# Seven conditional expert blocks, one after the other or one inside the other, on one core of Trainium2

## The chip, the core and the metric

The kernel runs on one core of one Trainium2 chip. A core has five engines with queues of their own: PE (TensorE, the matrix engine; PEld is its weight load), DVE (VectorE), ACT (ScalarE), POOL (GpSimd) and SP (SyncE). Each runs its own instruction list, and semaphores order them against each other. In this kernel SP issues the plain transfers; POOL issues the indirect ones, which take row numbers from a table. The metric is the device time in microseconds (us), the median of three runs; for the kernel before it is 813.92 us (813.45 to 814.21).

## The reference

Three layers on 4 x 576 = 2304 tokens of 512 numbers, in float32:

```python
q_s = softmax over the head dimension of q;  k_s = softmax over the sequence of k
kv = einsum('bhsd,bhse->bhde', k_s, v);  x = einsum('bhsd,bhde->bhse', q_s, kv)   # 4 x 8 heads x 64
x = (sigmoid(x @ w_gate) * (x @ w_val)) @ w_out                                   # 512 -> 1536 -> 512
logits = x @ w_gate2;  expert = argmax(logits);  gate = softmax(logits)[expert]   # 8 experts
# the first 576 tokens of an expert, in token order, are kept, the others give 0
out[i] = gate[i] * (relu(x[i] @ w1[expert]) @ w2[expert])                         # 512 -> 1024 -> 512
```

How many tokens an expert has is known only when the second layer is done. With the inputs used here four experts have tokens, and four have none.

## The kernel before

Every float32 product is made of three products of rounded parts (high x high, high x low, low x high), hence three matmul lines, 115 to 117, in the helper `mm3`, and "splits" (lines 134 and 135), in which ACT writes the rounded part and DVE or POOL the remainder.

The first two layers run over four blocks of tokens and write x to a buffer `x2d` in device memory. Beside the last block, tokens are routed: a table `tbl` in device memory holds, for each expert and slot, the token's number and its gate. POOL writes it with scatters (`scatter`, line 144), three for each block, the last three called by `rt["put"]()` in line 919. SP reads pieces of it back with `fetch` (lines 155 to 164).

The third layer is the subject. The expert with the most tokens goes first, outside any condition: 192 of its rows beside the last routing, then its last 384 rows. Their table is fetched into the tile `tb` by line 939, a step of the hidden chunk f = 3; the three scatters of the last block to the table are issued later, as one of the pieces in the list `weave`, which are called one by one between matmuls. The other seven follow in order of their number of tokens, each in a block of its own:

```python
for j in range(1, NE):
    with tc.If(nact > j):
        st, ew = body(j, st, ew)
```

`nact`, the number of experts that have tokens, is read by every engine from the tile `plan`. It is 4 here: the blocks j = 1, 2, 3 run, and j = 4 to 7 are passed over. `tc.If` makes a compare-and-branch on every engine, in the profile at line 1055. When the condition doesn't hold, the engine jumps to a small block that stands behind the body, the skip block: it waits for what the body before it left open, makes the semaphores' counts what they would be after the body (on POOL with INC_SWDGE_SEM), and branches on.

`body` (lines 1020 to 1052) multiplies 256 rows of one expert, and 320 more under an inner condition (line 1043), whose other side only splits weights. Inside, ACT makes the relu (line 235), DVE the low part of it (line 238), PE the second product into `yo`, ACT scales it by the gate (line 214), half tiles pass through a transfer to `z` (line 217), and POOL scatters the rows to the output (line 144). Beside this work SP loads the weights of the next expert into the staging tile `es` (lines 123 and 124), ACT, DVE and POOL split them into `eu`, SP fetches the next expert's table (lines 160 and 164), and POOL gathers its rows from `x2d` into `gr` (line 167).

Tiles come from pools: `hp` 4, `stg` 2, `psa` 5, `pso` 3, `grp` 7, `xgp` 2, `tbp` 2 of each kind; each call of `pool.tile` takes the next one and orders its users behind the last users of that place. The weights' `unit`s, six for an expert, are taken anew in every body. The program ends at line 1094, which is the closing barrier.

Of the kernel before, what the change touches and what calls it, by code (L numbers as in the profile page):

```python
# [8 lines left out]
F32 = mybir.dt.float32  # L9
F32R = mybir.dt.float32r  # L10
# [8 lines left out]
P = 128  # L19
# [19 lines left out]
SKIP = 8192  # L39
SPE = [mybir.EngineType.SP]  # L40

# The order in which the work up to the first pair of hidden chunks is issued, each engine's in turn: a step and
# what it is for (batch, tile or hidden chunk), with a star where VectorE takes it from its usual engine.
FIRST = """
lk0.0 lq0 km0.0 lk0.3 qm0 km0.3 lq3 ke0.0 ke0.3 lk0.2 qm3 lk0.1 qb0 qe0 kt0.3 km0.2 lk1 km0.1 lv0.0 ke0.2 qb3
qe3 lq1 qs0 qn0 kt0.0 lv0.3 kt0.2 ke0.1 kt0.4 qs3 km1.1 qt0 kc0.2 qn3 kc0.0 km1.2 kc0.4 kt0.1 kk0.0 kc0.3 qm1
# [21 lines left out]
go4.0 hl5.1* ac4.2 ac3.2* ac4.0*  # L68
"""
F64_MIN = struct.unpack("<f", struct.pack("<I", 897 << 20))[0]  # L70


def program(tc, ins, outs):
    nc = tc.nc
    ctx = ExitStack()
    with ctx:
# [76 lines left out]
            tc.add_to_no_dep_group(group, i.ins)  # L153

        def fetch(st, key, e, r0, k, rest=False):
            """The table's rows from r0 on: k to a partition, the rest's last half tile in both halves."""
            st[key] = t = tbp.tile([P, k + rest, 4], I32, name=key, tag=key[:2])
            t3 = tbl.rearrange("(e r) w -> e r w", e=NE)
            r1 = r0 + k * P
            nc.sync.dma_start(t[:, :k], t3[bass.ds(e, 1), r0:r1].rearrange("o (p k) w -> (o p) k w", k=k))  # L160
            if rest:
                for h in (0, HALF):
                    rows = t3[bass.ds(e, 1), r1 : r1 + HALF].rearrange("o p w -> (o p) w")
                    nc.sync.dma_start(t[h : h + HALF, k], rows)
# [21 lines left out]
            )  # L186

        def part(x, w, sizes, ew, t, ypool, ytag, hook, after):
            """The rows of one table for one expert. The high and low parts of a tile of half the rows fill the
            array's columns together; the low part's sums then move to the high part's partitions."""  # L190
            k, used = len(sizes), sum(sizes)
            full = used // P * P
            po, ys = [None] * k, [None] * k

            def second(f, h, i):
                n, sl = sizes[i], slice(i * P, i * P + sizes[i])
                w_hi, w_lo = ew[1, f][:, 0], ew[1, f][:, 1]
                if f == 0:
                    po[i] = pso.tile([P, 512], F32, name=f"yo{i}", tag="o")
                if n == P:  # L200
                    mm3(po[i], h[:, 0, sl], h[:, 1, sl], w_hi, w_lo, f == 0, f == 7)
                    return
                if f > 0:
                    nc.tensor.matmul(po[i][:n], h[:, 0, sl], w_lo, start=False, stop=False)
                nc.tensor.matmul(po[i], h[:, 0, used - n : used + n], w_hi, start=f == 0, stop=f == 7)
                if f == 0:
                    nc.tensor.matmul(po[i][:n], h[:, 0, sl], w_lo, start=False, stop=False)
                if weave:
                    weave.pop(0)()

            def emit(i):
                n = sizes[i]
                y = ypool.tile([P, DM], F32, name=f"y{i}", tag=ytag)
                nc.scalar.activation(y, po[i], AF.Copy, scale=t[:, i, 2:3].bitcast(F32))
                if n < P:
                    z = unit([P, DM], F32, f"z{i}") if ytag == "cv" else ypool.tile([P, DM], F32, name=f"z{i}", tag=ytag)
                    nc.sync.dma_start(z[:n], y[n:])
                    yield
                    nc.vector.tensor_tensor(y[:n], y[:n], z[:n], op=ALU.add)
                scatter(outs["out"], t[:n, i, 1:2], y[:n], NT, "out")  # L220

            hs = []
            for f in range(8):
                hook(f)
                ph = ps(f"ph{f}")[:, :w]
                w4 = ew[0, f].rearrange("p l (c m) -> p l c m", c=NC)
                for j, (l, r) in enumerate(((0, 0), (1, 0), (0, 1)) if f == 0 else ()):
                    for c in range(NC):
                        nc.tensor.matmul(
                            ph, w4[:, l, c], x[:, c, r], start=j + c == 0, stop=j == 2 and c == NC - 1  # L230
                        )
                for c in range(NC if f else 0):
                    mm3(ph, w4[:, 0, c], w4[:, 1, c], x[:, c, 0], x[:, c, 1], c == 0, c == NC - 1)
                h = hp.tile([P, 2, BLK], F32R, name=f"h3{f}", tag="h")
                nc.scalar.activation(h[:, 0, :used], ph[:, :used], AF.Relu)  # L235
                for dst, cols in ((h[:, 0, used : 2 * used - full], slice(full, used)), (h[:, 1, :full], slice(0, full))):
                    if cols.start < cols.stop:
                        nc.vector.scalar_tensor_tensor(  # L238
                            dst, ph[:, cols], 0.0, h[:, 0, cols].bitcast(F32), op0=ALU.max, op1=ALU.subtract
                        )  # L240
                hs.append(h)
                if 0 < f < 7:
                    for i in range(k):
                        second(f - 1, hs[f - 1], i)
                if f < 7:
                    after(f)
            half = sizes[-1] < P
            order = ([k - 1] if half else []) + list(range(k - half))
            for i in order[:2]:
                second(6, hs[6], i)  # L250
            after(7)
            after(8)
            out = [emit(i) for i in range(k)]
            for j, i in enumerate(order):
                second(7, hs[7], i)
                next(out[i], None)
                if j + 2 < k:
                    second(6, hs[6], order[j + 2])
            next(out[-1], None)

        with ExitStack() as s2:
# [247 lines left out]
            otile = {}  # L509

            def g2(b, fs, mode):
                """mode: add (whole sums to SBUF), open and close (a sum over two pairs in PSUM)"""
                order = [(tt, i) for tt in range(TPB) for i in range(2)]
                if b == NBLK - 1 and mode == "close":
                    order = [(tt, 0) for tt in range(TPB)] + [(tt, 1) for tt in range(TPB)]
                for tt, i in order:
                    if i == 0 and mode != "close":
                        otile[b, tt] = pso.tile([P, 512], F32, name=f"po{b}_{fs[0]}_{tt}", tag="o")
                    pair(b, tt, fs[i], i, mode != "close" and i == 0, mode != "open" and i == 1)
                    if i == 1 and mode != "open":  # L520
                        nc.vector.tensor_tensor(row(b, tt), row(b, tt), otile[b, tt], op=ALU.add)  # L521
                if fs[-1] == NFC - 1:
                    finish(b)
# [49 lines left out]
            nsum = {0: (5, 5, 5), 1: (5, 5, 5), 2: (5, 5, 5), 4: (5, 5)}  # L573

            def logits(b):
                """Queues the logits of block b: DVE sums nsum[b] products of a row, Pool and ScalarE the others."""
                lg_tile(b)
                for tt, n in enumerate(nsum[b]):
                    qd.extend((b, tt, e) for e in range(n))
                    qg.extend((b, tt, e) for e in range(n, NE))  # L580

            def slot(room, spare):
                """Fills the time that DVE (room, in products) and Pool (spare) have until the next pair's turn."""
                lg_sum(0)
                put = None
                busy = {x[0] for x in qd + qg}
# [315 lines left out]
            def last_rows():  # L902
# [12 lines left out]
                def end():  # L915
                    nc.vector.tensor_tensor(gidx, pi[:, :3], st0["tb5"][:, :, 0], op=ALU.add)
                    for i in range(3):
                        gather(st0, 2 + i, gidx[:, i : i + 1], w5[:, 0, i], P)
                    rt["put"]()

                weave.extend([lambda: None] + [lambda k=k: one(k) for k in range(3)] + [end])

            def after0(f):
# [12 lines left out]
                if f == 3:  # L936
                    last_rows()
                    ew_split(ew0, 7, both)
                    fetch(st0, "tb", rt["e0"], R0, 3)
                if f == 4:  # L940
                    rt["plan"] = make_plan()
                if f >= 4:
# [74 lines left out]

        nact = st.pop("nact")

        def body(j, st, ew):  # L1020
            more = j + 1 < NE
            cj = nc.values_load(plan[0:1, NE + j : NE + j + 1], min_val=0, max_val=NT)
            xb = unit([P, NC, 2, RB], F32R, "xb")
            nst, new = {}, {}

            def extra(f):
                if f == 0:
# [9 lines left out]

            half = work(new, nexp[j], range(4), (2, 4, 5, 6)) if more else {}
            part(st["xa"], RA, (P, P), ew, st["ta"], grp, "gr", *hooks(half, extra))
            if more:  # L1040
                for k in (3, 4, 5):
                    new["u", k] = unit([P, 3, 2, 512], F32R, f"eu{k}")
            with tc.If(cj > RA) as big:  # L1043
                half = work(new, nexp[j], range(4, 8), (1, 3, 5, 6)) if more else {}
                part(xb, RB, (P, P, HALF), ew, st["tb"], grp, "gr", *hooks(half))
# [5 lines left out]
                            w()  # L1051
            return nst, new

        for j in range(1, NE):
            with tc.If(nact > j):  # L1055
                st, ew = body(j, st, ew)


def layout(inputs):
# [38 lines left out]
```

## Time and profile before

| what | value |
|---|---|
| median of three runs (lowest, highest) | 813.92 us (813.45, 814.21) |
| profiled execution: span | 815.9 us |
| profiled execution: own time beside its span | none given |
| PE busy | 757.5 us (93%) |
| PE weight load busy | 689.0 us (84%) |
| DVE busy | 474.4 us (58%) |
| ACT busy | 293.0 us (36%) |
| POOL busy | 321.0 us (39%) |
| bytes moved | 72.62 MB, mean 89 GB/s |

The page comes from one profiled execution, whose time is not given apart from its span; the span is 2.0 us above the median of the runs. Busy times count work only: branches, waits on semaphores and the issue of transfers are not in them. They stand in the views of a line under the names PEldq, DVEq, ACTq, POOLq and SPq, the engines' queues. The granted clock PEclk is a share of full speed: 1.00 is 2.4 GHz.

### The profile page before, as it was taken

To read this page: it belongs to the slowest core of one execution; us is meant where nothing else is said; L and a number is where in the kernel's file an instruction comes from. 1 tells how busy PE (TensorE), PEld (TensorE's weight loads), DVE (VectorE), ACT (ScalarE), POOL (GpSimd) and SP (SyncE) were. 2 spreads that over 40 slices of the span, in tenths; PEclk is the share of its full clock that TensorE was granted. 3 is DMA by queue.
4 is the path that set the end of the run, shared out by engine and by line. 5 is a ranking of instruction groups with operands and counts; after the bars stand their busy time and mean duration, and the time that the engine had idled before them with its cause. 6 is when DMAs were issued, how large, how long until landed. Compare 5 with 4: busy or idle time off the path is not lost. (4 is left out here: it accounts for less than half of the span.)

```text
span 815.9 us, 11856 instructions
## 1 busy us (share of the span) xinstructions
PE 757.5 (93%) x4268; PEld 689.0 (84%) x4268; DVE 474.4 (58%) x933; ACT 293.0 (36%) x592; POOL 321.0 (39%) x309
## 2 busy tenths in 40 slices
PE   6989999999999999999997898989999999999980
PEld 5988998999999999999886787978798888888870
DVE  7999956344545445546889895587624422533330
ACT  6766733222222222222333332233235433523330
POOL 5472703222323223223466763462435423425220
PEclk9999999999999999999999898999999999999995
DMA  9951023101101011011211011124245523415311
GB/s 308 365 174 58 27 78 130 57 26 52 50 29 52 28 50 52 27 53 51 79 39 40 1 39 40 53 91 144 66 146 189 177 78 125 155 53 176 129 46 30
DMA packets 34942, 72.62 MB, mean 89 GB/s; under 512 B 6544, under 2 KB 8720, under 8 KB 34736
## 3 DMA queue, kind: packets, MB, share of 16 engines
q1 hardware_dynamic: 31152, 61.50, 22.7%
q0 software_dynamic: 3712, 10.13, 3.8%
q8 instruction: 42, 0.69, 0.4%
q14 instruction: 36, 0.29, 0.1%
HBM read 61.55 MB, written 9.55 MB: 87 GB/s over the span
## 5 line engine op out<-in xcount | busy, mean ns | idle before, releaser
L491 POOL TENSOR_TENSOR h<-sg,h 128x384 fp32r<-128x384 f32 x70 | 77.7, 1111 | 200.8 <-ACT h L487 194.6
L483 DVE TENSOR_TENSOR sg<-sg,pv 128x384 f32<-128x384 f32 x72 | 39.6, 551 | 103.2 <-PE pv L117 78.5
L115 PE MATMUL po<-w,h 128*128 128x512 f32 x216 | 88.4, 409 | 10.9 <-ACT h L487 10.9
L117 PE MATMUL pv<-xT,w 128*128 128x384 f32 x288 | 97.1, 337 | 1.5 <-POOL w L451 1.5
L115 PE MATMUL pg<-xT,w 128*128 128x384 f32 x288 | 98.0, 340 | 0.0
L115 PE MATMUL pv<-xT,w 128*128 128x384 f32 x288 | 97.7, 339 | 0.1
L116 PE MATMUL pv<-xT,w 128*128 128x384 f32 x288 | 96.8, 336 | 0.0
L116 PE MATMUL pg<-xT,w 128*128 128x384 f32 x288 | 96.7, 336 | 0.0
L117 PE MATMUL pg<-xT,w 128*128 128x384 f32 x288 | 96.4, 335 | 0.0
L117 PE MATMUL po<-w,h 128*128 128x512 f32 x216 | 89.4, 414 | 4.5 <-POOL h L491 4.4
L116 PE MATMUL po<-w,h 128*128 128x512 f32 x216 | 87.6, 406 | 0.0
L238 DVE SCALAR_TENSOR_TENSOR h<-ph,h 128x64 fp32r<-128x64 f32 (+2 forms) x96 | 31.3, 353 | 94.6 <-ACT h L235 87.5
L451 POOL TENSOR_TENSOR w<-cv,w 128x512 fp32r<-128x512 f32 x34 | 45.0, 1324 | 98.7 <-ACT w L447 97.7
L487 ACT CAST h<-sg 128x384 fp32r<-128x384 f32 x68 | 34.9, 514 | 132.9 <-DVE sg L483 125.0
L135 POOL TENSOR_TENSOR eu<-es,eu 128x512 fp32r<-128x512 f32 x34 | 44.4, 1310 | 87.1 <-ACT eu L134 80.9
L521 DVE TENSOR_TENSOR acc<-acc,po 128x512 f32<-128x512 f32 x78 | 52.8, 686 | 34.7 <-PE po L117 32.7
L479 ACT ACTIVATE sg<-pg 128x384 f32<-128x384 f32 x72 | 35.0, 486 | 102.8 <-PE pg L117 102.8
L235 ACT ACTIVATE h<-ph 128x256 fp32r<-128x256 f32 (+3 forms) x64 | 26.3, 411 | 109.0 <-PE ph L117 54.4
L135 DVE TENSOR_TENSOR eu<-es,eu 128x512 fp32r<-128x512 f32 x46 | 48.3, 1061 | 26.3 <-ACT eu L134 26.0
L115 PEld LDWEIGHTS po<-w,h 128*128 128x128 f32 x216 | 42.0, 194 | 21.3 <-ACT h L487 13.5
L557 DVE CUSTOM_DVE_ANT_0 jk<-acc,wgb 128x512 bf16<-128x512 f32 x55 | 58.8, 1069 | 1.5
L117 PEld LDWEIGHTS po<-w,h 128*128 128x128 f32 x216 | 42.3, 196 | 17.3 <-POOL h L491 7.4
(206 smaller groups left out, 1804.1 us busy)
## 6 DMA issues: line engine op xcount, KB each, us to landing
es<-in_w SPq DMA_DIRECT2D x80, 256.0 KB
s<-in_w SPq DMA_DIRECT2D x30, 512.0 KB
q<-in_q SPq DMA_DIRECT2D x18, 256.0 KB
x2d<-acc SPq DMA_DIRECT2D x6, 768.0 KB
kt<-in_kT SPq DMA_DIRECT2D x3, 1152.0 KB
vt<-in_v SPq DMA_DIRECT2D x3, 1024.0 KB
raw<-in_w SPq DMA_DIRECT2D x6, 512.0 KB
wgb<-in_wg SPq DMA_DIRECT2D x1, 2048.0 KB
```

Source lines behind the costliest of these rows:

```text
L115: nc.tensor.matmul(out, l_hi, r_hi, start=start, stop=False)
L116: nc.tensor.matmul(out, l_hi, r_lo, start=False, stop=False)
L117: nc.tensor.matmul(out, l_lo, r_hi, start=False, stop=stop)
L135: engines[(i + f) % 2].tensor_tensor(u[:, 1], s[:, i], u[:, 0].bitcast(F32), op=ALU.subtract)
L238: nc.vector.scalar_tensor_tensor(dst, ph[:, cols], 0.0, h[:, 0, cols].bitcast(F32), op0=ALU.max, op1=ALU.subtract)
L451: two[eng].tensor_tensor(w[:, i, 1, :], ld.pop(("c", f, i))[0], w[:, i, 0, :].bitcast(F32), op=ALU.subtract)
L479: nc.scalar.activation(pr, gt.pop(("g", b, f)), AF.Sigmoid)
L483: nc.vector.tensor_tensor(pr, pr, gt.pop(("v", b, f)), op=ALU.mult)
L487: alt[eng](h[:, 0], gt["r", b, f])
L491: two[eng].tensor_tensor(h[:, 1], gt.pop(("r", b, f)), h[:, 0].bitcast(F32), op=ALU.subtract)
L521: nc.vector.tensor_tensor(row(b, tt), row(b, tt), otile[b, tt], op=ALU.add)
L557: nc.vector.tensor_tensor_reduce(junk, row(b, tt), rt["wg"][:, e, :], 1.0, 0.0, op0=ALU.mult, op1=ALU.add, accum_out=rt["lg", b][:, tt, e ...
```

## The change

Four things differ. (1) The seven blocks stand one inside the other: `chain` opens the condition of number j, writes its body and then, still inside, calls itself for j + 1. (2) The tiles of the third layer are taken once, ahead of the blocks, and come round as fixed lists (`Ring`, and `Tables` for the two kinds of table tile), as many as the pools had; the weight units are two fixed sets of six, used in turn; the tile for the later rows is `xb1`, always the same. (3) The fetch of the first expert's last table rows is moved from the step of chunk f = 3 to behind `rt["put"]()`. (4) Comments are gone, by which the line numbers move.

```diff
+class Ring:
+    def __init__(self, tiles):
+        self.tiles, self.n = list(tiles), 0
+
+    def tile(self, shape, dt, name, tag):
+        self.n += 1
+        return self.tiles[(self.n - 1) % len(self.tiles)]
+
+class Tables:
+    def __init__(self, ta, tb):
+        self.of = {"ta": ta, "tb": tb}
...
                         gather(st0, 2 + i, gidx[:, i : i + 1], w5[:, 0, i], P)
                     rt["put"]()
+                    fetch(st0, "tb", rt["e0"], R0, 3)
...
                     last_rows()
                     ew_split(ew0, 7, both)
-                    fetch(st0, "tb", rt["e0"], R0, 3)
...
+        def ring(pool, n, shape, dt, tag, *first):
+            more = [pool.tile(shape, dt, name=f"{tag}r{i}", tag=tag) for i in range(n)]
+            return Ring([*more, *first])
+        sets = [
+            {k: u for k, u in ew.items() if k[0] == "u"},
+            {("u", k): unit([P, 3, 2, 512], F32R, f"ev{k}") for k in range(6)},
+        ]
+        xb1 = unit([P, NC, 2, RB], F32R, "xb1")
+        hp = ring(hp, 4, [P, 2, BLK], F32R, "h")
+        stg = ring(stg, 2, [P, 2, 512], F32, "stg")
...
+        tbp = Tables(ring(tbp, 1, [P, 2, 4], I32, "ta", st["ta"]), ring(tbp, 1, [P, 3, 4], I32, "tb", st["tb"]))
...
-            xb = unit([P, NC, 2, RB], F32R, "xb")
-            nst, new = {}, {}
+            xb = xb1
+            nst, new = {}, dict(sets[j % 2])
...
-            if more:
-                for k in (3, 4, 5):
-                    new["u", k] = unit([P, 3, 2, 512], F32R, f"eu{k}")
...
-        for j in range(1, NE):
+        def chain(j, st, ew):
             with tc.If(nact > j):
-                st, ew = body(j, st, ew)
+                nst, new = body(j, st, ew)
+                if j + 1 < NE:
+                    chain(j + 1, nst, new)
+
+        chain(1, st, ew)
```

In the order of the instructions the change is seen at three places. The first is POOL's list where one of the seven blocks ends and the next begins. Before, there stand the last two splits of a body, the end of the inner condition, the skip block of the outer one (line 1055: one instruction of the kind that holds INC_SWDGE_SEM, and a branch), the compare of the next block and the first lines of its body. DMAHW, DMASW and names of engines are semaphores.

```order
L135 TENSOR_TENSOR eu_7868<-es_8137,eu_7868 128x512 [waits DMAHW6_49,Activation_49]
L1043 ISA [waits DMASW7_49,DMASW6_49,DMASW5_49]
L1043 UNCONDITIONAL_BRANCH
L1055 ISA [waits Pool_49,Pool_sequencer_49,DMASW4_49,DMASW5_49,DMASW3_49,DMASW6_49,DMASW2_49,DMASW7_49,DMASW1_49,DMASW0_49]
L1055 UNCONDITIONAL_BRANCH
L1055 COMPARE_AND_BRANCH
L1022 TENSOR_LOAD plan
```

And now, the end of POOL's list: the skip blocks of the nested conditions, those of the inner ones first, and behind them the closing barrier.

```order
L1089 ISA [waits Pool_49,Pool_sequencer_49,DMASW4_49,DMASW5_49,DMASW3_49,DMASW6_49,DMASW2_49,DMASW7_49,DMASW1_49,DMASW0_49]
L1089 UNCONDITIONAL_BRANCH
L1089 ISA [waits Pool_49,Pool_sequencer_49,DMASW4_49,DMASW5_49,DMASW3_49,DMASW6_49,DMASW2_49,DMASW7_49,DMASW1_49,DMASW0_49]
L1089 UNCONDITIONAL_BRANCH
L1132 ISA [waits barrier_Pool_Activation_PE_DVE_SP_gather]
```

The skip block, an ISA instruction and a branch, stood behind each body; now all seven stand together at the end of the list, two of them shown here.

The second place is PE's list. Before, where a body ends, its skip block (one branch with waits) and the next compare follow the last product.

```order
L116 MATMUL yo_7915<-eu_7291,h_8082 128x512
L117 MATMUL yo_7915<-eu_7291,h_8082 128x512
L1043 UNCONDITIONAL_BRANCH
L1043 UNCONDITIONAL_BRANCH [waits PE_49]
L1055 UNCONDITIONAL_BRANCH [waits PE_49,PE_sequencer_49]
L1055 COMPARE_AND_BRANCH
L1022 TENSOR_LOAD plan
```

Now, the end of PE's list, behind the last body's last product.

```order
L135 MATMUL or_5854<-eu_5806,hr_5846 128x512
L136 MATMUL or_5854<-eu_5806,hr_5846 128x512
L1077 UNCONDITIONAL_BRANCH
L1077 UNCONDITIONAL_BRANCH [waits PE_49]
L1089 UNCONDITIONAL_BRANCH [waits PE_49,PE_sequencer_49] x7
```

The seven branches that stood each behind its own body stand behind one another at the end.

The third place is SP's list around the moved fetch, where the first expert's 192 rows are multiplied: `es` are weights of an expert, `tb<-tbl` the fetch, and the load of `plan` follows it. Before:

```order
L124 DMA es_5096<-in_w 128x512
L160 ISA
L160 DMA tb<-tbl 128x12
L217 DMA z_5349<-y_5347 64x512 [waits Activation_49]
L973 TENSOR_LOAD plan [waits DVE_49]
```

Now:

```order
L143 DMA es_5096<-in_w 128x512
L179 ISA
L179 DMA tb<-tbl 128x12 [waits DMASW6_49]
L236 DMA z_5349<-y_5347 64x512 [waits Activation_49]
L992 TENSOR_LOAD plan [waits DVE_49]
```

On SP the fetch has kept its neighbours and has a wait for one of POOL's transfers.

## Rows read from the trace of the kernel before

**Rows 1.** first line of the page

```profile
span 815.9 us, 11856 instructions
```

**Rows 2.** stages: the bodies, the end (columns in the first line)

```profile
core 0: us, PE busy (x) PEld busy (x) DVE busy (x) ACT busy (x) POOL busy (x), PEclk, DMA share, GB/s
735.40:790.80 55.40, 54.52 (x326) 48.08 (x325) 19.56 (x38) 20.76 (x42) 20.27 (x18) 1.00 0.37 122
790.80:801.40 10.60, 2.27 (x10) 1.50 (x8) 0.68 (x1) 2.06 (x3) 2.90 (x3) 0.71 0.32 87
801.40:815.90 14.50, 0.00 (x0) 0.00 (x0) 0.00 (x0) 0.00 (x0) 0.00 (x0) 0.50 0.04 7
```

**Rows 3.** line 1055 from 790 us (ns min/median/max, start us)

```profile
L1055 PEldq COMPARE_BRANCH  x4: 4761/4855/4924, 790.9 to 806.5; - x4
...
L1055 POOLq COMPARE_BRANCH  x4: 45/48/50, 796.5 to 808.1; - x4
L1055 POOLq INC_SWDGE_SEM  x4: 1353/1353/1357, 801.5 to 808.8; - x4
```

**Rows 4.** line 1055 on POOL, four stretches from 797, 803, 806 and 808.2 us

```profile
L1055 POOLq EVENT_SEMAPHORE  x4: 17/43/43, 800.9 to 801.4; - x4
...
L1055 POOLq COMPARE_BRANCH  x1: 50/50/50, 802.8 to 802.8; - x1
...
L1055 POOLq EVENT_SEMAPHORE  x6: 17/30/43, 803.3 to 803.8; - x6
...
L1055 POOLq COMPARE_BRANCH  x1: 45/45/45, 805.2 to 805.2; - x1
...
L1055 POOLq EVENT_SEMAPHORE  x6: 17/30/43, 806.2 to 806.7; - x6
...
L1055 POOLq COMPARE_BRANCH  x1: 45/45/45, 808.1 to 808.1; - x1
...
L1055 POOLq EVENT_SEMAPHORE  x5: 17/43/43, 808.3 to 808.7; - x5
```

**Rows 5.** line 1094, the end of the program

```profile
L1094 SPq EVENT_SEMAPHORE  x14: 17/28/1201, 810.1 to 815.9; - x14
...
L1094 POOLq DRAIN  x3: 46/107/4960, 810.1 to 815.7; - x3
...
L1094 PEldq DRAIN  x2: 8/8/8, 811.8 to 815.4; - x2
```

**Rows 6.** end of the chain of work (start us, us, what)

```profile
796.59 0.92 POOL out L144
```

**Rows 7.** waits of SP's queue from 780 us (total, times, longest)

```profile
SPq L1094 <- PEq L1055: 1.2, 1, 1.2
```

**Rows 8.** DMA queues, 796 to 799.2, then 799.2 to 801 us

```profile
q0 software_dynamic: 122, 0.38, 39.8%
q8 instruction: 2, 0.03, 7.8%
...
q0 software_dynamic: 9, 0.02, 5.6%
```

**Rows 9.** line 1055 on DVE, 796.9 to 799.8 us

```profile
L1055 DVEq EVENT_SEMAPHORE  x3: 21/21/21, 796.9 to 799.5; - x3
L1055 DVEq COMPARE_BRANCH  x2: 56/56/56, 797.0 to 799.6; - x2
```

**Rows 10.** waits of PE in the three bodies, 624 to 791 us

```profile
PE yo L115 <- ACT h L235: 1.4, 2, 0.8
PE yo L115 <- issue: 0.9, 1, 0.9
```

**Rows 11.** tbl on POOL, z on SP, SP's waits, 580 to 640 us

```profile
L144 POOL DMA_INDIRECT tbl<-ent,si x3: 977/1005/1024, 585.0 to 587.7; - x3
...
L217 SPq DMA_DIRECT2D z<-y x1: 507/507/507, 592.1 to 592.1; - x1
...
SPq L217 <- ACT y L214: 19.1, 1, 19.1
```

More of the change, by code (lines that the diff above doesn't have):

```diff
@@ L70, with tile @@
 F64_MIN = struct.unpack("<f", struct.pack("<I", 897 << 20))[0]
+class Ring:
[7 more added lines that the diff above has]
+        self.of = {"ta": ta, "tb": tb}
+    def tile(self, shape, dt, name, tag):
+        return self.of[tag].tile(shape, dt, name, tag)
 def program(tc, ins, outs):
@@ L1018, in program @@
         nact = st.pop("nact")
+        def ring(pool, n, shape, dt, tag, *first):
[8 more added lines that the diff above has]
+        stg = ring(stg, 2, [P, 2, 512], F32, "stg")
+        psa = ring(psa, 5, [P, 512], F32, "a")
+        pso = ring(pso, 3, [P, 512], F32, "o")
+        grp = ring(grp, 7, [P, DM], F32, "gr")
+        xgp = ring(xgp, 1, [P, NC, 2, RA], F32R, "xa", st["xa"])
+        tbp = Tables(ring(tbp, 1, [P, 2, 4], I32, "ta", st["ta"]), ring(tbp, 1, [P, 3, 4], I32, "tb", st["tb"]))
         def body(j, st, ew):
```

## The prediction

> **What bounds the kernel now.** I read the stages first, then the end of the chain of work, then the branch line 1055 and the closing line 1094. The span is 815.9 us [rows 1]. In the expert bodies TensorE is the limit: the third body takes 55.4 us and PE is busy 54.5 of them at a granted clock of 1.00, which is 2.4 GHz, while the DMA engines are busy a third of the time [rows 2]. In all three bodies PE waits for ACT or for instructions 2.3 us in total [rows 10]. Whatever the change does inside a body has only these 2.3 us to win.
>
> The last 14.5 us, from 801.4 on, hold no compute at all: every engine's busy time is zero [rows 2]. The chain of work that ended last stops with the third output scatter of the last body, which starts at 796.6 and takes 0.9 us [rows 6]; everything after 797.5 is branches, waits and the closing barrier. There the reader sees four not-taken decisions of line 1055, each of them on PE and on POOL, so four of the seven experts are skipped and three run (one hot expert ahead of them) [rows 3].
>
> On POOL each skip is a few waits, one INC_SWDGE_SEM of 1.35 us and a branch. The first skip cannot begin before the scatters have landed: its waits end between 800.9 and 801.4 [rows 4]. The first of the four INCs starts at 801.5, the last at 808.8 [rows 3]. POOL then starts a DRAIN at 810.1, which is the 4.96 us one, so it ends at 815.1, and 0.8 us of barrier close the span [rows 5, 1]. TensorE needs 4.76 to 4.92 us for each of its four skips, because the branch itself takes that long [rows 3]; it reaches its own drain at 811.8 [rows 5], 3.3 us before POOL's DRAIN ends. So POOL's queue is the end of the kernel, PE's the next one behind it.
>
> **The change part by part.**
>
> Nesting. Compare number four still fails, its skip block runs, and the branch at the end of that block leads to the end of the program, past the skip blocks of numbers three, two and one. Three of four skips go, on all engines. On POOL from the start of the first INC (801.5) to the start of the DRAIN (810.1) is 8.6 us; of that 1.35 for one INC stay and the exit branch. What a branch costs on POOL until the next instruction: from 802.8 to 803.3, 0.5; from 805.2 to 806.2, 1.0; from 808.1 to 808.3, 0.2 [rows 4]. I take 0.3 for the exit. 8.6 - 1.35 - 0.3 = 7.0 us.
>
> The jump to the skip block becomes longer: before, POOL leaps over one body, now over four. The nearest row for a leap that leaves what is loaded is DVE's, whose branch at 797.0 is followed by the next event only at 799.4 or 799.5: 2.4 us [rows 9]; PE's dearest is 4.9 [rows 3]. POOL branches at 796.5 and could not go on before 801.4 anyway; 796.5 + 4.9 = 801.4. So between 0 and 2.4 us are hidden behind the landing of the scatters, and even PE's price just fits. Cost 0. If that cover were gone, up to 2.4 (estimate from DVE's row).
>
> The landing itself. From 796 to 799.2 the scatter queue moves 122 packets, beside two instruction packets (0.03 MB), which I put down to PE's second skip, since its four skips lie 5.2 us apart from 790.9 on [rows 3]; from 799.2 to 801 only nine stragglers are left [rows 8]. With PE's second skip gone, those two loads are gone at this place, while POOL's longer jump may put one in. If the stragglers were behind them, the wait ends near 799.5 instead of 801.4, 1.9 us earlier; if not, 0. I take 0.9, the middle, since the rows name no cause.
>
> The DRAIN. Four are not to be seen, only one long one (4.96 us) and two short ones (0.05 and 0.11) [rows 5]. If it is a fixed price of the first drain after indirect DMAs it stays; if it works off what four INCs left, three quarters or all of it goes. I take it as fixed, because each INC stands in the trace as finished before the next instruction. If it shrinks, SP is next: after POOL's last INC it has 14 event waits, 810.1 to 812.0, of which 1.2 were PE's skip [rows 5, 7], so 0.7 us, then the 0.8 of the barrier.
>
> PE. Its one remaining skip ends its long branch at 790.9 + 4.8 = 795.7 and its drain follows there, if the exit is cheap, or at about 800.6 if the exit costs another 4.9. Both are before POOL. SP, DVE and ACT have one skip left, too, and wait for POOL.
>
> The Trainium skill ("Runtime: NRT & Kernel Launch", Instruction fetch mechanics) says that prefetch is sequential and that a taken branch to a target outside the loaded window stalls until that code has been fetched. PE's branch of 4.8 us against POOL's 0.05 on the same line agrees with it [rows 3], and it speaks against nesting: every engine's jump now goes further. By that rule alone the exit could stall as well, which is the second rival below.
>
> Tiles taken once. The pools of stage 3 and the weight tiles become fixed lists. The same tiles are used in the same rotation (4, 2, 5, 3, 7, and two sets of six weight units), so the matrix work and the splits are unchanged; what changes is the list of semaphores before an instruction. SP's weight loads now wait for each half of the staging tile by itself, which can only be earlier than waiting for both. All this sits beside PE, which is busy 98% of a body. Bounds: all 2.3 us of PE's waits go, or three more such waits of 0.9 come [rows 10]. I take 0.
>
> The moved fetch. The last 384 rows of the first expert's table are fetched by SP where the three scatters to the table have been issued, and wait for them. The last scatter starts at 587.7 and takes 1.0 [rows 11]. Landing: from the output scatters above at most 801.4 - 797.5 = 3.9 us, so 592.6 at the latest; with the fetch's issue SP is free at 593.0 at the latest. What is queued behind it on SP is the z transfer at 592.1, for which SP sat waiting 19.1 us [rows 11], then the loads of the plan and the next expert's weights. The entries of the table are 16 bytes a row instead of 2 KB, so I expect the landing near 590 and no delay: 0, at worst 0.9. The fetched rows are used only where that expert's outputs are scaled, at its end. POOL's scatters lose a wait for the fetch that was over anyway.
>
> **Sum.** 7.0 + 0.9 + 0 + 0 = 7.9 us off the profiled span of 815.9: 808.0. The page gives no other time for that execution; the median of the three runs, 813.92, is 2.0 below the span. I take the difference over to the median: 813.9 - 7.9 = 806.0 us. Its own range is 804 to 808: landing 0 to 1.9, exit 0.1 to 1.0, bodies about 1 either way.
>
> **Rivals.**
>
> The DRAIN shrinks with the skips. For: it is longer than any other drain, and four INCs precede it. Against: the INCs look finished. Then the end is the last INC, 801.5 - 0.9 + 1.35 = 801.9, plus 0.7 and 0.8, and 0.2 for the short drain and the exit: 803.6 in place of 815.9, so 12.3 less: 801.6.
>
> The exit pays a fetch on POOL. For: PE's branches [rows 3]. Against: the skip blocks passed over are a few instructions each, and POOL's branches cost 0.2 to 1.0 [rows 4]. 4.8 instead of 0.3: 810.5 (with DVE's 2.4: 808.1).
>
> The nest doesn't do what it says: the engines walk through the skip blocks of numbers three, two and one. Then four INCs are still paid, and only PE's long branches go, which POOL covered: 813.9 - 0.9 = 813.0 at best, within what can be told. For: the three blocks do stand between. Against: each ends in its own branch.
>
> Slower: the new waits hit the bodies. Mechanism: a relu on ACT comes late and PE's second product waits for it, as it did three times in the bodies, at most 0.9 us each [rows 10]. SP's first loads of a body no longer wait for the z transfer and so run into the gathers and output scatters at the start of a body. From nine more such waits (9 x 0.9 = 8.1) it outweighs the end, three a body. At five a body, 13.5 us: 813.9 - 7.9 + 13.5 = 819.5. Against: the products, splits and transfers of a body are the same in kind and number, and the tiles come round as often as before; only 2.3 us of such waits are there now.
>
> **How the numbers follow.** Forecast 0.60, shrinking DRAIN 0.18, dear exit 0.10, walking through 0.05, slower bodies 0.05, and 0.02 for the rest. The range 801.0 to 811.0 takes in the forecast, nearly all of the second and of the third case; left out are the last ones and the tails. What a measurement can tell from no change is about 0.2%, 1.6 us. Faster by more: 0.60 + 0.18 + 0.10 and a part of the rest, 0.90. Within: most of walking through, 0.05. Slower: 0.05.
>
> **What would show it.** In the profile after: line 1089 in the tail with one INC_SWDGE_SEM and one compare on POOL instead of four, one branch of 4.8 us on PE, and an empty stage after the last landing of about 7 us instead of 14.5. The DRAIN's length decides between forecast and first rival, the gap between POOL's only INC and its DRAIN is the exit. Body lengths of 55.4 to 55.8 and PE's waits of 2.3 us should stand; a longer body, or a z transfer later than 592.1 us, would prove the part on tiles or on the fetch wrong. Two or more INCs on POOL in the tail would prove the main step wrong.

## The result and the profile after

The changed kernel takes 804.6 us (median of four runs, 804.01 to 805.22) against 813.84 us (813.45 to 814.21): ratio 0.9891, 95% interval [0.9879, 0.9903], so 9.2 us less. The forecast was 806.0.

First the stages, with the same cuts by content as in [rows 2]: the third body, from there to the start of the INC_SWDGE_SEM on POOL, and the rest.

```profile
span 803.4 us, 11808 instructions
...
733.00:787.20 54.20, 54.20 (x327) 48.18 (x326) 19.56 (x38) 20.87 (x42) 20.79 (x18) 1.00 0.38 124
787.20:795.70 8.50, 2.25 (x10) 1.49 (x8) 0.68 (x1) 2.06 (x3) 3.10 (x3) 0.76 0.36 104
795.70:803.40 7.70, 0.00 (x0) 0.00 (x0) 0.00 (x0) 0.00 (x0) 0.00 (x0) 0.50 0.00 1
```

The stage without compute is 7.7 us long where it was 14.5 [rows 2], the one ahead of it 8.5 where it was 10.6. The next lines are the skip (line 1089, formerly 1055) from 780 us and the program's end (line 1132, formerly 1094).

```profile
L1089 POOLq EVENT_SEMAPHORE  x6: 17/30/43, 793.2 to 795.7; - x6
L1089 PEldq COMPARE_BRANCH  x2: 188/1855/3522, 787.1 to 791.0; - x2
...
L1089 POOLq COMPARE_BRANCH  x2: 38/44/50, 791.6 to 797.2; - x2
L1089 POOLq INC_SWDGE_SEM  x1: 1371/1371/1371, 795.7 to 795.7; - x1
...
L1132 POOLq DRAIN  x3: 46/107/5047, 797.6 to 803.2; - x3
...
L1132 PEldq DRAIN  x2: 8/8/8, 791.2 to 802.9; - x2
```

One INC where there were four [rows 3], one long branch on PE where there were four (the second, 0.19 us, is the exit), and the DRAIN on POOL of the same length as before [rows 5]. PE reaches its own drain at 791.2, long before POOL. The last output scatter (line 163, formerly 144) is issued at 792.5, and 0.92 us later that is done; POOL's waits for the scatters end at 795.7, just ahead of the INC.

```profile
L163 POOL DMA_INDIRECT out<-grr,tb x3: 917/994/1190, 789.8 to 792.5; - x3
```

To compare ends I measure from PE's last product to the end of the span, the tail. Its start is the last number of a row of line 136 (line 117 before), the third product of a tile; first the row of after, from 786 us on, then that of before, from 789 us on.

```profile
L136 PE MATMUL or<-eu,hr x4: 389/392/400, 786.5 to 789.1; 128*128 128x512 f32 x4
```

```profile
L117 PE MATMUL yo<-eu,h x4: 389/392/400, 790.1 to 792.7; 128*128 128x512 f32 x4
```

Before, the tail is 815.9 - 792.7 = 23.2 us, now 803.4 - 789.1 = 14.3: 8.9 us less (unrounded 23.3 and 14.4, as in the table below). The other 3.6 us by which the two spans differ lie ahead of it: product for product, PE is 1.7 us earlier when the first body begins, and 1.9 more by its last product. In the bodies it has one wait, where [rows 10] have three (from 620 to 788 us).

```profile
PE or L136 <- DVE hr L257: 1.7, 1, 1.7
```

That part is not to be had in the median: 8.9 and 3.6 make 12.5, and the medians differ by 9.2. In every run whose span is listed the time is 1.7 to 1.9 us above it (805.22 and 803.4 in the traced one of after), so the traced execution of before had, by estimate, about 817.7 us, 3.9 above its median. What the tail gained is enough to explain the medians.

### The profile page after: what moved, and what is told of

Its sections match the earlier page's. It is cut to its first block, busy times and chain, and to the rows that moved or that the text cites. A ratio compares the mean times of both kernels' runs of the same rounds, so it can differ in the third digit from the quotient of the medians.

```text
span 803.4 us, 11808 instructions
## 1 busy us (share of the span) xinstructions
PE 755.3 (94%) x4268; PEld 688.5 (86%) x4268; DVE 473.4 (59%) x933; ACT 293.7 (37%) x592; POOL 322.7 (40%) x309
## 4 chain that ended last, share of the span: by engine, by line
PE 69%; DVE 18%; issue 7%; POOL 2%; ACT 2%; DMA 1%; SPq 0%; DVEq 0%; POOLq 0%; ACTq 0%
PE po L136 5%; PE po L135 5%; PE po L134 5%; DVE jk L576 5%; PE pv L136 5%; PE pv L134 5%; PE pv L135 5%; PE pg L134 4%; PE pg L135 4%; PE pg L136 4%; PE ar L134 2%; PE ar L136 2%; PE ar L135 2%; PE or L136 2%; PE or L134 2%
## 5 line engine op out<-in xcount | busy, mean ns | idle before, releaser
L257 DVE SCALAR_TENSOR_TENSOR hr<-ar,hr 128x64 fp32r<-128x64 f32 (+1 forms) x72 | 23.4, 354 | 80.5 <-ACT hr L254 79.7
L136 PEld LDWEIGHTS pv<-xT,w 128*128 128x128 f32 x288 | 54.6, 189 | 2.3 <-POOL w L470 2.3
L134 PEld LDWEIGHTS pg<-xT,w 128*128 128x128 f32 x288 | 54.2, 188 | 1.8 <-issue 0.3
L135 PEld LDWEIGHTS pg<-xT,w 128*128 128x128 f32 x288 | 54.1, 188 | 1.4
```

Of the source, the lines that this page charges most:

```text
L134: nc.tensor.matmul(out, l_hi, r_hi, start=start, stop=False)
L135: nc.tensor.matmul(out, l_hi, r_lo, start=False, stop=False)
L136: nc.tensor.matmul(out, l_lo, r_hi, start=False, stop=stop)
L257: nc.vector.scalar_tensor_tensor(dst, ph[:, cols], 0.0, h[:, 0, cols].bitcast(F32), op0=ALU.max, op1=ALU.subtract)
```

## The experiments

The experiments were run in four sets: one holds the rows from "flat, fixed tiles" to "fetch only", two those from "after, set two" to "six and one", three the two DRAIN rows behind them, four the last two rows. Every set has its own runs of the kernel before beside it; the ratios refer to these. The landing and tail in the row of before are those of the first pair. "Landing" is the time from the end of the last output scatter's issue to the start of the first INC on POOL. Tail and landing are read from each kernel's trace.

| run | skips | time, us (lowest to highest) | ratio to before [95%] | landing | tail |
|---|---|---|---|---|---|
| before | 4 | (sets: 815.96, 813.53, 815.83, 814.0) | 1 | 4.0 | 23.3 |
| after, first pair | 1 | 804.6 (804.01 to 805.22) | 0.9891 [0.9879, 0.9903] | 2.3 | 14.4 |
| flat, fixed tiles | 4 | 815.94 (813.99 to 817.95) | 0.9989 [0.9967, 1.0011] | 3.4 | 23.0 |
| two nests | 2 | 818.01 (815.23 to 820.34) | 1.0001 [0.998, 1.0022] | 3.8 | 20.0 |
| fetch back | 1 | 812.64 (805.92 to 816.15) | 0.9948 [0.992, 0.9976] | 2.4 | 14.7 |
| fetch only | 4 | 816.73 (812.87 to 820.7) | 0.9997 [0.9971, 1.0022] | 3.5 | 22.8 |
| after, set two | 1 | 805.74 (804.79 to 806.24) | 0.9905 [0.9893, 0.9918] | 2.3 | 14.6 |
| DRAIN in the body | 1 | 813.74 (812.25 to 815.66) | 1.0001 [0.9993, 1.001] | - | 11.5 |
| near skip | 2 | 806.35 (806.19 to 806.91) | 0.9913 [0.99, 0.9926] | 2.7 | 16.1 |
| six and one | 2 | 809.04 (807.16 to 810.13) | 0.9941 [0.9928, 0.9953] | 3.9 | 18.0 |
| DRAIN in the skip | 1 | 809.72 (804.13 to 810.18) | 0.9912 [0.9882, 0.9943] | - | 11.8 |
| flat, DRAIN in the skip | 4 | 812.76 (810.73 to 815.89) | 0.9958 [0.9935, 0.998] | - | 19.9 |
| after, set four | 1 | 805.89 (804.72 to 806.64) | 0.9903 [0.9886, 0.9919] | 2.2 | 14.5 |
| DRAIN in the skip, set four | 1 | 802.6 (801.36 to 804.64) | 0.9868 [0.9848, 0.9888] | - | 12.0 |

The tails of one kernel agree within some tenths from chip to chip. The times do not: in sets one and three, on other chips than sets two and four, even the kernel before spreads over 10 us (812.0 to 822.9). So the end is judged by tails, and times are compared within a set.

**1. Flat, fixed tiles** (e1).

```diff
-        def chain(j, st, ew):
-            with tc.If(nact > j):
-                nst, new = body(j, st, ew)
-                if j + 1 < NE:
-                    chain(j + 1, nst, new)
-        chain(1, st, ew)
+        for j in range(1, NE):
+            with tc.If(nact > j):
+                st, ew = body(j, st, ew)
```

> The changed kernel with the seven blocks one after the other again; tiles taken once and the moved fetch stay. Theory A (the gain is the three skips that fell away, with the earlier landing behind PE's second skip): everything that the end gained is lost again, 804.6 + 8.9 = 813.5 us, tail from PE's last product to the end 23 us, four INC_SWDGE_SEM on POOL from about 6 to 16 us after that product. Rival B (fixed tiles give 3.6 us in the bodies, as PE's steps in the two profiles differ): 813.8 - 3.6 = 810.2 us, no late relu in the bodies.

The time is that of the kernel before, and so is the tail, 23.0 us with four INCs. Theory A holds; B, 3.6 us by the fixed tiles, would be a ratio near 0.9956, which the interval excludes.

**2. Two nests** (e2), numbers 1 to 4 and 5 to 7.

```diff
-        chain(1, st, ew)
+        st, ew = chain(1, 4, st, ew)     # chain(j, last, ...) ends with `last`
+        chain(5, NE - 1, st, ew)         # and gives back its last st, ew
```

> The changed kernel with two nests, numbers 1 to 4 and numbers 5 to 7, one behind the other: two skips are paid, number 4 and number 5. Theory A (each skip has its own price on POOL's queue): one more skip, 1.4 for the INC and about 1.0 around it, so 804.6 + 2.3 = 806.9 us. Rival C (what the end gained is the landing of the scatters, which is late as soon as a second long branch on PE fetches instructions): the landing goes back as well, 804.6 + 2.3 + 1.7 = 808.6 us.

The tail is 20.0 us, 5.6 more than with one nest, more than either had said. Its skips, on line 1089:

```profile
L1089 PEldq COMPARE_BRANCH  x3: 188/3376/5242, 795.8 to 799.8; - x3
...
L1089 POOLq INC_SWDGE_SEM  x2: 1357/1357/1357, 805.9 to 810.5; - x2
```

PE makes a second long leap, the landing is late again by 1.5 us (C), and from INC to INC POOL needs 4.7 us. Of these 2.6 are its second leap, over three bodies, from the branch at 807.4 to the next event at 810.0:

```profile
L1089 POOLq EVENT_SEMAPHORE  x6: 17/30/43, 810.0 to 810.4; - x6
...
L1089 POOLq COMPARE_BRANCH  x2: 38/44/50, 807.2 to 807.4; - x2
```

In the changed kernel such a leap is there too, but it passes while the scatters are still landing. The time, 818.01, is no better than that of the kernel before: what the tail gained, 3 us, was lost ahead of it.

**3. Fetch back and 4. fetch only** (e3, e4): the moved fetch taken out of the changed kernel, and put alone into the one before.

```diff
                     rt["put"]()
-                    fetch(st0, "tb", rt["e0"], R0, 3)
...
                     ew_split(ew0, 7, both)
+                    fetch(st0, "tb", rt["e0"], R0, 3)
```

> The changed kernel with the fetch of the last table rows back in the step of chunk f = 3, ahead of the last scatters to the table, so those rows hold what stood there before. Theory A: nothing, 804.6 us within 0.8. Rival D (the moved fetch lets the half tile's transfer start 1.5 us earlier, 590.6 in place of 592.1): 806.1 us.

> The kernel before with the fetch moved behind the last scatters to the table and nothing else. Theory A: 813.8 us within 0.8, four skips at the end. Rival D: 812.3 us.

Alone the fetch moves nothing that can be told (0.9997; the interval would allow some 2 us either way). Without it the nested kernel keeps its tail, 14.7 us, but has only 0.5% in the time. Where its traced execution lost is seen in the stretch from 737 to 760 us, first of this kernel, then of after:

```profile
737.00:760.00 23.00, 19.90 (x127) 17.52 (x126) 7.71 (x13) 7.45 (x16) 11.80 (x11) 0.93 0.57 178
```

```profile
737.00:760.00 23.00, 23.00 (x150) 20.42 (x149) 10.53 (x18) 9.97 (x22) 12.60 (x11) 1.00 0.66 217
```

PE stood still once for 3.1 us: a relu on ACT came late, behind a wait of 6.2 us whose releaser the trace doesn't name ("remote"), and the granted clock fell with it. The missing name may be a lost record: the traces of sets one and three and of before hold about a tenth fewer semaphore records than the others (5721 here, 6393 in after).

```profile
ACT hr L254 <- remote: 8.9, 2, 6.2
```

The two nests of the same set have this stop too (3.8 us on the same line), with the fetch moved; the changed kernel in sets two and four hasn't. So the stop is not bound to the fetch. One execution without the moved fetch took 805.92, as little as the changed kernel in sets two and four; rival E of experiment 5 (the moved fetch is needed for the gain) falls. D falls by the traces: the half tile's transfer goes 0.02 to 0.03 us after ACT's scaling ends in those of before, after, e3 and e4 alike, wherever the fetch stands.

What goes with this loss is the nest, on some chips. Against what their tails gained, the three nested kernels of sets one and three (two nests, fetch back, DRAIN in the skip) are each some 5.3 us too slow in the median; the flat ones there 0.3 to 1.3, the nested ones of sets two and four, without the DRAIN in the body, at most 0.9 (the intervals of sets one and three are some 2 us either way). The changed kernel itself was not run on those two chips, and what makes that relu late stays open.

**5. The changed kernel again** (e5, and e11 below).

> The changed kernel itself, timed beside the others of this set. Theory A (the end is worth 8.4 to 8.9 us, the rest is scatter of PE's waits in the bodies): about 9 us below the kernel before of the same set, tail from PE's last product to the end 14.4 to 14.7 us. Rival E (the moved fetch is needed for the gain, since with the fetch ahead the nested kernel had only 3.3 us): the same 9 us, but with PE's waits in the bodies well below the 5.9 us of that kernel in every execution; if the gain here is only 3 to 5 us, E falls and the nested bodies themselves are slower by some us.

0.9905 and 0.9903, 7.8 and 8.1 us: the gain repeats where the bodies are undisturbed.

**6. A DRAIN in each body** (e6).

```diff
                 part(xb, RB, (P, P, HALF), ew, st["tb"], grp, "gr", *hooks(half))
+                nc.gpsimd.drain()
```

> The changed kernel with one DRAIN on POOL behind the last output scatter of each of the bodies. Theory A (5 us is the price of a DRAIN that comes after indirect transfers, each time anew): each body's DRAIN takes about 5 us on POOL and hides there; in the last body it starts 4.4 us after PE's last product and ends at 9.4, then waits, the INC of 1.4, and the closing DRAIN is short, 0.1 to 0.5: the end at about 9.4 + 0.3 + 1.4 + 0.5 + 0.3 + 0.8 = 12.7 us after PE, so 1.7 us less than the changed kernel, 802.9. Rival F (the INC is what the closing DRAIN works off): the DRAIN in the body is short, the closing one stays at 5 us and the time stays. Rival G (every DRAIN costs 5 us, whatever is ahead of it): both take 5 us, tail 9.4 + 0.3 + 1.4 + 0.5 + 5.0 + 0.8 = 17.4 us, 3.0 us more, 807.6.

The DRAINs of the three bodies (line 1080), the skip's INC (line 1090) and the closing DRAINs (line 1133):

```profile
L1080 POOLq DRAIN  x3: 4424/6202/6369, 684.4 to 803.8; - x3
...
L1090 POOLq INC_SWDGE_SEM  x1: 168/168/168, 811.0 to 811.0; - x1
...
L1133 POOLq DRAIN  x3: 40/55/107, 811.4 to 812.5; - x3
```

A DRAIN of 4.4 to 6.4 us stands wherever indirect transfers came ahead, the closing one is then 0.06 us, and, unexpected, the INC takes 0.17 us in place of 1.37. F and G fall. The tail is 11.5 us where A had 12.7; the shorter INC makes that difference. The DRAIN itself ran earlier than A had it, from 2.4 to 6.9 us after PE's last product, and the INC still began at 9.7; what held POOL between them stays open. But A's "hides there" was wrong: at a body's start POOL's gathers are queued behind the DRAIN, and PE waited for them.

```profile
PE ar L200 <- DMA grr<-x2d,tb: 4.2, 1, 4.2
PE ar L200 <- DMA grr<-x2d,tbr: 3.7, 1, 3.7
```

After each of these stops PE runs for some 3 us at a granted clock of 0.50 (columns as in [rows 2]; the stop of 3.7 us is shown, the other has the same from 755.3 to 758.5), so two stops cost more than the tail gave.

```profile
691.70:695.40 3.70, 0.02 (x1) 0.00 (x0) 0.00 (x0) 0.00 (x0) 2.68 (x3) 0.98 0.45 145
695.40:698.60 3.20, 3.18 (x15) 3.19 (x16) 0.69 (x1) 0.59 (x1) 2.56 (x4) 0.50 0.51 156
```

**7. A near skip** (e7): one more condition behind the nest, with a body of a few instructions that does not run here.

```diff
         chain(1, st, ew)
+        with tc.If(nact > 5):
+            g = grp.tile([P, DM], F32, name="g", tag="gr")
+            p = psa.tile([P, 512], F32, name="p", tag="a")
+            gather({}, 0, dropi[:, 0:1], g, P)
+            nc.tensor.transpose(p[:, :P], g[:, :P], ident)
...
```

> The changed kernel with one more condition behind the nest that does not hold here; its body is small (one gather, one transpose, two copies, one transfer), so the second skip is a leap over a few instructions. Theory C (the scatters land late because the second leap over a whole body makes PE fetch instructions in that time): landing as in the changed kernel, 2.3 to 2.4 us after the last scatter, PE's second branch well below 1 us, and the second skip costs an INC and its waits, 2.3 us: tail 14.5 + 2.3 = 16.8 us, 806.9 us. Rival H (a second skip of whatever length delays the landing by its semaphores): landing 3.4 to 3.9 us, tail 18.3 us.

**8. Six and one** (e8): two nests again, numbers 1 to 6 and number 7.

> The changed kernel with number 7 taken out of the nest and put behind it: two skips, number 4 out of the six and then number 7, a leap over one body. Theory C: PE's second branch again 4.5 to 5 us, the landing late, 3.4 to 3.9 us after the last scatter; on POOL the second leap goes over one body, as in the kernel before, so INC to INC 2.4 to 2.9 us (4.7 where the leap went over three bodies): tail 14.5 + 1.4 + 2.7 = 18.6 us. Rival I (a leap's price on POOL doesn't depend on its length): INC to INC 4.7 us, tail 20.0 us.

The near skip, its nest (line 1089) and the condition behind it (line 1095):

```profile
L1089 PEldq COMPARE_BRANCH  x2: 188/2050/3913, 786.4 to 790.6; - x2
...
L1089 POOLq INC_SWDGE_SEM  x1: 1367/1367/1367, 795.2 to 795.2; - x1
...
L1095 PEldq COMPARE_BRANCH  x1: 248/248/248, 790.9 to 790.9; - x1
...
L1095 POOLq INC_SWDGE_SEM  x1: 1334/1334/1334, 797.2 to 797.2; - x1
```

Six and one, line 1089:

```profile
L1089 PEldq COMPARE_BRANCH  x3: 188/3526/5462, 787.9 to 792.0; - x3
...
L1089 POOLq INC_SWDGE_SEM  x2: 1353/1360/1367, 798.2 to 800.6; - x2
```

Both pay two skips. With the near one, PE's second branch takes 0.25 us, the landing 2.7 and the tail 16.1; with the far one 5.46, 3.9 and 18.0. On POOL INC to INC is 2.0 and 2.4 us, not 4.7, so I falls: over three bodies the leap cost more than over one. C holds and H falls: counted from PE's last product, the INC of the near skip starts at 6.9 us, as in the three runs of the changed kernel (6.7 to 6.9), that of six and one at 8.4.

The transfers' own records say the same. The last packet of the output scatters ends 5.9 to 6.2 us after PE's last product in every kernel with one far leap, the near skip among them, and 7.2 to 8.0 us after it in every kernel with two or four. In those the instruction queue q8, the one of [rows 8], carries two packets beside the scatters, from 2 us after PE's last product on, and the later one ends at 6.0 to 7.3; in the others one, over by 4.4. So late landing and a second load of code go together. That the load delays the scatters' packets, and not something else in those leaps, is argued, not shown; nor is it shown whose leap it is, as the second leap goes on all engines at once.

**9. One DRAIN in the skip** (e9, e12), where POOL only waits for the landing.

```diff
-            with tc.If(nact > j):
+            with tc.If(nact > j) as run:
                 nst, new = body(j, st, ew)
                 if j + 1 < NE:
                     chain(j + 1, nst, new)
+            with run.Else():
+                nc.gpsimd.drain()
```

> The changed kernel with one DRAIN on POOL in the other arm of each of the seven conditions, so that it runs only where an expert is passed over, ahead of that skip's waits and INC. Theory J (a DRAIN of 4.4 to 5.0 us is paid once after indirect transfers, wherever it stands, and an INC behind it takes 0.17 us): the DRAIN starts about 5 us after PE's last product, when POOL's leap and the last scatter are over, ends at 9.4 to 10.0, behind the landing at 6.9; INC 0.2, exit 0.4, closing DRAIN below 0.1: tail 11.5 to 12.2 us in place of 14.5, 802.2 to 803.3 us, or 2.4 to 3.0 us below the changed kernel (ratio to the kernel before 0.987). Rival K (the DRAIN waits until the scatters have landed): it ends at 6.9 + 5.0 = 11.9, tail 13.8 us, 0.7 us less than the changed kernel.

The DRAIN in the skip (line 1094), the INC, and the closing DRAINs (line 1134):

```profile
L1094 POOLq DRAIN  x1: 5113/5113/5113, 794.8 to 794.8; - x1
...
L1089 POOLq INC_SWDGE_SEM  x1: 168/168/168, 800.5 to 800.5; - x1
...
L1134 POOLq DRAIN  x3: 34/107/156, 801.1 to 802.0; - x3
```

It starts 4.4 us after PE's last product and runs beside the landing: tail 11.8 us, J holds and K falls. The time of that set is 809.72. The traced execution took 804.13, the other six 808.6 to 810.2, so where these lost is not seen; hence a last set with the changed kernel beside it.

> The changed kernel once more, beside the next one on the same chip. In set two it stood at 0.9905 of the kernel before; the same is expected, 0.989 to 0.992, where the bodies are undisturbed, tail 14.4 to 14.7 us.

> The version with one DRAIN in the skip, on the same chip as the changed kernel. Theory J: tail 11.8 us as in its first run, so 2.6 to 2.8 us (0.33%) below the changed kernel of this set in the median. Rival O (what the DRAIN saves at the end is given back in the bodies, since its one undisturbed time of the last set, 804.1, stood beside six of 808.6 to 810.2): the medians of the two are equal or this one is the longer, with PE's last product later by 3 us or more than in the changed kernel of this set.

802.6 against 805.89 us: 3.3 us less, and every run of the one is below every run of the other; ratio to before 0.9868 [0.9848, 0.9888]. This version beats both kernels; rival O falls.

**10. Flat, with the DRAIN** (e10): the loop of experiment 1 with the two added lines of experiment 9.

> The seven blocks one after the other (fixed tiles, moved fetch), with the same DRAIN on POOL in each skip. Theory L (PE's queue is the next bound behind POOL's): POOL's first skip ends near 10.5 us after PE's last product, the next three cost about 1.2 us and their leaps, 14 to 17; PE needs four branches of 4.5 to 5.1 us one after the other, the last ends at about 18.7 to 19 us, and SP's closing waits and the barrier make the tail 20 to 20.5 us, 2.5 to 3 us below the 23.0 of the same kernel without the DRAIN. Rival M (POOL stays the bound, the DRAINs only add): tail 23 us or more. Rival N (the queue of PE doesn't matter): tail about 16 to 18 us.

The skips (line 1089) and the end (line 1130), where POOL's and PE's own parts are done:

```profile
L1089 PEldq COMPARE_BRANCH  x4: 4562/4858/4974, 789.1 to 804.4; - x4
...
L1089 POOLq INC_SWDGE_SEM  x4: 146/152/158, 801.8 to 806.3; - x4
...
L1130 POOLq DRAIN  x3: 34/34/107, 806.4 to 810.6; - x3
...
L1130 PEldq DRAIN  x2: 8/8/8, 809.8 to 810.4; - x2
```

POOL is done at 806.4 and PE at 809.8: L holds, M and N fall. PE's four leaps are the bound behind POOL's queue, tail 19.9 us. So the DRAIN alone shortens the flat kernel's tail by 3.1 us (23.0 to 19.9), and DRAIN and nest together by 11.2 (to 11.8).

## Why the prediction was right

Against the traced pair, term by term:

- Three skips fewer on POOL, 7.0 us. From the first INC to the long DRAIN it was 8.7 us unrounded, now 795.75 to 797.56, 1.8: 6.9 us. The exit took 0.4 where 0.3 was taken. With one INC on POOL, walking through the other skip blocks falls.
- The landing, 0.9 us as the middle between 0 and 1.9: this term was too small. The first INC stood 8.8 us after PE's last product, now 6.7: 2.1 us, 1.7 of them landing, near the range's upper end of 1.9, the other 0.4 because the last scatter itself is issued earlier. The middle was taken for want of a cause; experiments 7 and 8 give a part of it: the landing is early where no second far leap follows.
- The longer leap, 0 us: on POOL the branch at 791.6 is followed by the next event at 793.2, while the last scatter is still issued, and the waits end at 795.7. The cover named was there. Uncovered it is 2.6 us over three bodies (experiment 2), close to the 2.4 of DVE's row.
- The DRAIN, taken as a fixed price of the first one after indirect transfers: 5.05 us, as before. The shrinking DRAIN falls. Its ground, that INC and DRAIN have to do with one another, was half right: an INC behind a DRAIN is short (0.17 us against 1.37). Of the fourteen waits that this rival counted on SP from 810.1 to 812.0, two are the barrier's, at 815.3 and 815.9; its 0.7 us stands.
- PE, one leap and a cheap exit: 3.5 us, where 4.8 was expected, and 0.19. The dear exit falls, on POOL too (0.4). The rule of the Trainium skill that was weighed there ("Runtime: NRT & Kernel Launch", Instruction fetch mechanics) agrees with PE's branches in these runs: 0.25 us for a near leap, 3.4 to 5.5 for far ones. The skip blocks passed over at the exit were near; how much code an engine holds, no run shows.
- Fixed tiles, 0: the interval of experiment 1 allows at most 2.7 us and includes none. The rival of slower bodies did not come in the runs of the first pair. On the chips of sets one and three it came in part: some 5.3 us in nested kernels (experiments 3 and 4), in the traces of two nests and fetch back by a late relu, as the rival has it.
- The moved fetch, 0: it was issued at 589.8 us, as estimated, and the z transfer went at 590.6, not later than its 592.1 [rows 11]; alone it is 0.9997. It bears on what is read, not on the time: before, the fetch went at 572.7 us, ahead of the three scatters from 585.0 on.

The tail gained 8.9 us (6.9 and 2.1, less 0.1 by which the DRAIN was longer) where 7.9 was forecast, and 804.6 against 806.0 us is mostly the landing's 1.2 us. Taking the forecast off the median and not off the span was needed: the traced execution of before was a long one, and the two spans differ by 12.5.

## What to carry to other kernels

A skipped block is not free: count, for each engine, the leaps over code that isn't run and the queue that pays for them one after the other, and let one exit pass all that follow. An edit at the end of a program is judged by the tail of the trace, not by spans of two executions, and its times on more than one chip: on two of them the nested bodies gave a part of the gain back. Where an engine waits at the end anyway, put the work there that would otherwise come after, as the DRAIN in the skip; put the same work in front of gathers that the next stage needs and it costs more than it gives.

## What the runs showed of the hardware

- POOL's DRAIN after indirect transfers took 4.4 to 6.6 us once, and 0.03 to 0.16 when no such transfer lay between it and the one before.
- INC_SWDGE_SEM took 1.33 to 1.37 us, and 0.15 to 0.17 behind a DRAIN.
- A compare whose branch goes over one or more whole bodies took PE 3.4 to 5.5 us, over a few instructions 0.19 to 0.25.
- The last packet of the output scatters ended 5.9 to 6.2 us after PE's last product with one far leap behind it, 7.2 to 8.0 with two or four.
- A stop of PE of 3.7 us was followed by some 3 us at a granted clock of 0.50, which is 1.2 GHz (experiment 6).
